# Attention scores of neighbouring blocks in two PSUM banks, the odd one with its heads' partition halves exchanged

## The chip, the cores and the metric

The kernel runs on one core of a Trainium2 chip. The metric is the time of one execution in microseconds of the device. Three runs of the kernel before took 499.46, 500.41 and 501.45 us; the median is 500.41 us.

## The reference

```python
# attention: 4 batches, 8 heads, 576 positions, 64 features a head
scores = scale * np.matmul(q, k.transpose(0, 1, 3, 2))
mask_plain = (rel >= 0) & (rel < 32)                          # heads 0 to 3
mask_dil = (rel >= 0) & (rel < 128) & (rel % 4 == 0)          # heads 4 to 7
scores = np.where(masks, scores, -1e9)
attn = softmax(scores); attn_out = attn @ v
# dense layer on the 2304 tokens of 512 features
h = x @ w_in; g = h - np.tanh(h); x = g @ w_out
# soft mixture of 8 experts with 4 slots each
logits = x @ phi
slot_input = softmax(logits, axis=0).T @ x
slot_out[e] = np.maximum(slot_input[e] @ w1[e], 0) @ w2[e]
out = softmax(logits, axis=1) @ slot_out
```

All data are float32. (`softmax` stands here for the subtraction of the maximum, exp, and the division by the sum plus 1e-9.)

## The kernel before

Everything runs in an order written out by hand: each engine executes its instructions in the order in which the program emits them. TensorE (PE) multiplies, ScalarE (ACT) and VectorE (DVE) read the results out of PSUM, GpSimd (POOL) works on SBUF alone, and all DMAs are issued from the SP queue.

**Attention.** The windows are narrow, so only blocks of the score matrix are computed. A step `i` handles a pair of heads (p) and a third (u) of their positions: 12 steps a batch, `PO = (2, 3, 0, 1)`, so the six dilated steps come first and the six plain ones after. A dilated step has 4 blocks of 48 queries by 80 keys, a plain step 3 blocks of 64 by 96 (`shape`, L279). One step passes through

- `emit_qk` (L247): transposes of q and k (L267) and their copies into `qk`, several of them for each pair of heads;
- `emit_scores` (L283): for each block c and each head x of the pair one matmul (L305). Head x has its 64 features in partitions 64x to 64x+63 and puts its scores into the same half of the partitions of one PSUM tile; the blocks lie side by side in the columns. For batches 0 and 1 (`by_pe`, `MASKPE = 2`) one bf16 matmul (L291) has put the mask there first and L305 adds to it, and the maximum (L314) and exp (L317, one ACT instruction a block, which also reads out the row sums) read PSUM. For batches 2 and 3 DVE adds the mask on the way to SBUF (L311), and the maximum and exp read SBUF;
- `emit_norm` (L323): reciprocals of the sums on DVE (L326, L328) and a multiplication on POOL (L329);
- `emit_trans` (L332): one transpose a block (L338) and a copy to SBUF by ACT (L97);
- `emit_pv` (L343): the product with v (L359, two column halves, one for each head), then ACT casts it to `xhi` (L97), DVE subtracts to get `xlo` (L391), and some tiles leave a remainder that is copied (L97).

**PSUM.** The pool `ps_m` has five banks under the tag `mm`; `mm(shape)` (L78) takes one of them. q/k transposes, scores, score transposes, products with v, transposes of g and several smaller things all go through these five. `ps_h` has two banks for h.

**Dense layer.** h of a chunk of 512 tokens (here: of a batch) is made of three products in fp32r for each quarter of the features (L503 to L505), then tanh on ACT (L509), a subtraction on DVE (L512), the logits (L518, four tiles of 32 output partitions) and a transpose of g (L537).

**Order.** Batches 0 and 1 of attention, the conversion of the weights (POOL L430, DVE L441 to L446, PE L468 to L492) and the first chunk of h are sorted by due times that stand at the top of the file; this fills the time to about 157 us. Extra matmuls (`warm`, L195) stand behind the first four scores. Then chunks 1 to 3 follow in a loop over eight pairs s of feature tiles. Attention of batch 2 is laid into chunk 1 and that of batch 3 into chunk 2 by the class `Attn`, pair by pair: `turn(s)` emits q/k transposes and the score transposes of the pair before, `score` the scores of steps 2s and 2s+1, `norms` their normalisation, and `values(s)` the products with v of the steps 2s-2 and 2s-1:

```python
                emit_tanh(pb, gs[b])
                if an:
                    an.score(2 * s)
                emit_sub(pb, gs[b])
                if an:
                    an.score(2 * s + 1)
                    an.norms(s)
                    an.values(s)
```

After that come the experts.

Of the kernel before, what the change touches and what calls it, by code (L numbers as in the profile page):

```python
# [13 lines left out]
ACTF = mybir.ActivationFunctionType  # L14
ALU = mybir.AluOpType
AX = mybir.AxisListType
# [43 lines left out]
def moe_kernel(ctx: ExitStack, tc: tile.TileContext, q, k, v, w_in, w_out, phi, w1, w2, out):  # L60
    nc = tc.nc
# [16 lines left out]
    def mm(shape):  # L78
        return ps_m.tile(shape, F32, tag="mm", name="mm")
# [46 lines left out]
    id2 = cpart(64).bitcast(BF16)[0:64].rearrange("p (a k) -> p a k", a=2)  # L126
# [156 lines left out]
    def emit_scores(b, i):  # L283
        p, u = PO[i // 3], i % 3
        nb, nq, nk = shape(i)
        ps = mm([128, nb, nk])
        mask = mask_d[:, (0, 4, 2)[u]:(4, 8, 6)[u]] if nb == 4 else mask_p[:, min(u, 1):min(u, 1) + 3]
        by_pe = b < MASKPE
        nr = nq if by_pe else 64
        if by_pe:  # L290
            nc.tensor.matmul(  # L291
                ps.rearrange("p c k -> p (c k)"), lhsT=id2.rearrange("p a k -> p (a k)"),
                rhs=mask[0:64].rearrange("p c k -> p (c k)"), start=True, stop=True,
            )
        for c in range(nb):
            for x in range(2):
                if nb == 4:

                    r2, qi = divmod(2 * u + c // 2, 3)
                    q0 = 288 * (c % 2) + 144 * r2  # L300
                    q0, k0 = q0 + nq * qi, q0 + max(0, nq * qi - 32)
                else:
                    q0, k0 = nq * (nb * u + c), max(0, nq * (nb * u + c) - 32)
                r = slice(64 * x, 64 * x + 64)
                nc.tensor.matmul(  # L305
                    ps[64 * x:64 * x + nr, c, :], lhsT=qT[b, p][r, q0:q0 + nr], rhs=kT[b, p][r, k0:k0 + nk],
                    start=not by_pe, stop=True, skip_group_check=True,
                )
        pr = prs.next()[:, 0:nb * nk].rearrange("p (c k) -> p c k", c=nb)
        if not by_pe:  # L310
            nc.vector.tensor_tensor(out=pr, in0=ps, in1=mask, op=ALU.add)  # L311
            ps = pr
        nm = tiny("nm", 4, 3)[:, 0:nb]
        nc.vector.tensor_reduce(out=nm, in_=ps, op=ALU.max, axis=AX.X, negate=True)  # L314
        sm = tiny("smm", 4, 3)[:, 0:nb]
        for c in range(nb):
            nc.scalar.activation(  # L317
                out=pr[:, c, :], in_=ps[:, c, :], func=ACTF.Exp, bias=nm[:, c:c + 1],
                accum_out=sm[:, c:c + 1],
            )  # L320
        sc_s[b, i] = (pr, sm)
# [21 lines left out]
    def emit_pv(b, i):  # L343
        p, u = PO[i // 3], i % 3
        nb, nq, nk = shape(i)
        if i == 0:
            xhi[b] = unit("xhi", [128, KT, 512], F32R)
            xlo[b] = unit("xlo", [128, KT, 512], F32R)
        pt = sc_pt.pop((b, i))
        o = mm([128, 192])  # L350
        for n0 in range(nb):
            for hh in range(2):
                if nb == 4:
                    m, x = divmod(n0, 2)
                    r2, qi = divmod(2 * u + m, 3)
                    n, c, col = 3 * (2 * r2 + x) + qi, 2 * m + hh, 96 * x + nq * m
                else:
                    n, c, x, col = nb * u + n0, n0, hh, nq * n0
                nc.tensor.matmul(  # L359
                    o[64 * hh:64 * hh + 64, col:col + nq], lhsT=vt[b, p](n, hh),  # L360
                    rhs=pt[:, c, 64 * x:64 * x + nq], start=True, stop=True,
                )
        hi, lo, rem = xhi[b][:, p, :], xlo[b][:, p, :], xrem[:, p, 64 * b:64 * b + 64]
        pieces, rems = [], []
        if p >= NP // 2:
            if u == 0:
                halves2 = lambda t: t.rearrange("p (l y) -> p l y", l=2)
                pieces.append((halves2(o), lambda t: halves2(t[:, 0:288])[:, :, 0:96]))
            elif u == 1:
                pieces.append((  # L370
                    o.rearrange("p (l m i) -> p m l i", l=2, m=2),
                    lambda t: t[:, 96:480].rearrange("p (m l i) -> p m l i", m=2, l=4)[:, :, ::3, :],
                ))
            else:
                pieces.append((o[:, 0:96], lambda t: t[:, 336:432]))
                pieces.append((o[:, 96:128], lambda t: t[:, 480:512]))
                rems.append((o[:, 128:192], rem))
        else:
            ov = o.rearrange("p (i r) -> p r i", r=4)
            pieces.append((ov[:, 0:3, :], lambda t: t[:, 0:432].rearrange("p (r i) -> p r i", r=3)[:, :, 48 * u:48 * u + 48]))  # L380
            if u == 0:
                pieces.append((ov[:, 3, :], lambda t: t[:, 432:480]))
            elif u == 1:
                pieces.append((ov[:, 3, 0:32], lambda t: t[:, 480:512]))
                rems.append((ov[:, 3, 32:48], rem[:, 0:16]))
            else:
                rems.append((ov[:, 3, :], rem[:, 16:64]))
        for src, f in pieces:
            copy(ENGS["hi"][min(b, 2)], f(hi), src)
        for src, f in pieces:  # L390
            nc.vector.tensor_tensor(out=f(lo), in0=src, in1=f(hi).bitcast(F32), op=ALU.subtract)  # L391
        for src, dst in rems:
            copy(ENGS["rem"][min(b, 2)], dst, src)
# [379 lines left out]
    with tc.manual_schedule():  # L773
# [71 lines left out]
        for ch in range(1, 4):  # L845
# [13 lines left out]
            for s in range(NFT // 2):  # L859
                a, b = 2 * s, 2 * s + 1  # L860
                pa, gs[a] = emit_h(xh, xl, a), gring.next()
                emit_tanh(pa, gs[a])
                emit_sub(pa, gs[a])

                if s:
                    emit_gT(ch, a - 2, gs[a - 2])
                    emit_gT(ch, a - 1, gs[a - 1])
                elif ch > 1:
                    last_posts()
                if s or ch == 1:  # L870
                    sm_one()
                if an:
                    an.turn(s)
                pb, gs[b] = emit_h(xh, xl, b), gring.next()
                emit_tanh(pb, gs[b])
                if an:
                    an.score(2 * s)
                emit_sub(pb, gs[b])
                if an:
                    an.score(2 * s + 1)  # L880
                    an.norms(s)
                    an.values(s)
                if s:
                    emit_logits(ch, a - 1, gs[a - 1])
                emit_logits(ch, a, gs[a])
                sm_one()
                room[0] += sum(ROOM.get((ch, f), 0) for f in (a, b))
                load_experts()
# [183 lines left out]
```

## Time and profile before

| what | value |
| --- | --- |
| median of three runs | 500.41 us (499.46 to 501.45) |
| the profiled execution | 501.07 us, span 499.3 us |
| TensorE busy | 470.8 us (94% of the span) |
| DVE, ACT, POOL busy | 222.9, 236.0, 83.6 us |
| L305, score matmuls | 672 instructions, mean 254 ns each, 36.0 us busy |
| mean granted TensorE clock | 0.96 |

The profile is of one execution. Times are in us from the start of the span; L305 is line 305 of the kernel. Matmuls overlap each other, so the time of one matmul is its latency; what a group costs is seen where the chain that ended last runs through it. PE is the matmul side of TensorE, PEld its weight loads. The granted clock is the share of the full TensorE clock.

### The profile page before, as it was taken

The numbers are of one execution on the slowest core, as the hardware profiler recorded it, in microseconds if no ns is written. First come the engines' busy times: TensorE is split into PE (matmuls) and PEld (weight loads), VectorE is DVE, ScalarE is ACT, GpSimd is POOL, SyncE is SP. The second block draws the span as 40 slices with busy tenths as digits, with TensorE's granted clock in tenths as the row PEclk, the third lists the DMA queues.
The fourth block names the chain that finished last, engine by engine and source line by source line (L and its number), as shares of the span: only waits on it lengthen the run. The fifth ranks groups of instructions, "written<-read, shape, count | busy, mean of one in ns | idle before, by whom it ended". The sixth has DMA issues, their size and how long they took to land.

```text
span 499.3 us, 11253 instructions
## 1 busy us (share of the span) xinstructions
PE 470.8 (94%) x4531; PEld 351.4 (70%) x4531; DVE 222.9 (45%) x558; ACT 236.0 (47%) x763; POOL 83.6 (17%) x99
## 2 busy tenths in 40 slices
PE   6989888999999999999999899999999999999981
PEld 4767676877777867888787678877678869845430
DVE  1787888954754445543252454332221223232132
ACT  3857536575655464665365356543132323313121
POOL 3463444432341010111011011100000000010000
PEclk9967768999999999999999999999999999999996
DMA  9997799444145401222320100209600259899938
GB/s 247 277 262 258 258 336 269 151 117 121 35 139 123 96 3 39 76 59 49 81 44 1 37 1 2 86 4 390 254 29 0 85 180 402 304 389 410 409 146 334
DMA packets 60740, 81.14 MB, mean 163 GB/s; under 512 B 35600, under 2 KB 39440, under 8 KB 60688
## 3 DMA queue, kind: packets, MB, share of 16 engines
q1 hardware_dynamic: 60688, 80.42, 49.7%
q8 instruction: 36, 0.59, 0.5%
q14 instruction: 16, 0.13, 0.1%
HBM read 71.50 MB, written 8.91 MB: 161 GB/s over the span
## 4 chain that ended last, share of the span: by engine, by line
PE 85%; DVE 6%; ACT 4%; issue 1%; DMA 1%; POOL 0%; POOLq 0%; ACTq 0%; DVEq 0%
PE h L503 14%; PE h L505 13%; PE h L504 13%; PE mm L305 6%; PE mm L537 5%; PE lg L518 4%; PE mm L359 4%; PE mm L338 4%; PE mm L635 3%; PE mm L267 3%; PE h L686 3%; PE y L711 3%; ACT mem L317 2%; PE warm L200 1%; PE mm L468 1%; PE mm L479 1%
## 5 line engine op out<-in xcount | busy, mean ns | idle before, releaser
L503 PE MATMUL h<-xhi,whi 128*128 128x512 f32 x256 | 107.1, 418 | 0.0
L505 PE MATMUL h<-xhi,wlo 128*128 128x512 f32 x256 | 101.0, 395 | 0.0
L504 PE MATMUL h<-xlo,whi 128*128 128x512 f32 x256 | 100.8, 394 | 0.0
L509 ACT ACTIVATE mem<-h 128x512 f32<-128x512 f32 x56 | 33.4, 596 | 83.7 <-PE h L505 83.7
L512 DVE TENSOR_TENSOR mem<-h,mem 128x512 f32<-128x512 f32 x56 | 38.6, 689 | 73.6 <-ACT mem L509 73.4
L329 POOL TENSOR_TENSOR mem<-mem 128x320 f32<-128x320 f32 (+1 forms) x48 | 34.5, 718 | 195.7 <-DVE mem L328 132.7
L503 PEld LDWEIGHTS h<-xhi,whi 128*128 128x128 f32 x256 | 48.8, 191 | 13.3 <-issue 5.0
L505 PEld LDWEIGHTS h<-xhi,wlo 128*128 128x128 f32 x256 | 48.5, 189 | 10.9
L504 PEld LDWEIGHTS h<-xlo,whi 128*128 128x128 f32 x256 | 48.9, 191 | 8.4
L97 ACT COPY g<-mm 128x512 f32<-128x512 f32 x72 | 40.2, 596 | 12.0 <-PE mm L550 4.8
L317 ACT ACTIVATE mem<-mm,mem 128x80 f32<-128x80 f32 (+1 forms) x84 | 26.8, 330 | 30.1 <-DVE mem L314 30.1
L305 PE MATMUL mm<-qk 64*64 64x96 f32 (+2 forms) x672 | 36.0, 254 | 2.1 <-DVE qk L97 2.0
L317 ACT ACTIVATE mem<-mem 128x80 f32<-128x80 f32 (+1 forms) x84 | 29.9, 357 | 16.5 <-DVE mem L314 14.5
L305 PEld LDWEIGHTS mm<-qk 64*64 64x64 f32 (+1 forms) x672 | 29.0, 139 | 10.6 <-issue 5.6
L97 ACT COPY mem<-mm 80x448 f32<-80x448 f32 (+4 forms) x64 | 26.7, 442 | 10.1 <-DVE xlo L391 6.5
L338 PE MATMUL mm<-mem 112*80 112x112 f32 (+1 forms) x168 | 25.4, 279 | 5.0 <-POOL mem L329 2.8
L311 DVE TENSOR_TENSOR mem<-mm,mem 128x320 f32<-128x320 f32 (+1 forms) x24 | 11.3, 470 | 41.8 <-PE mm L305 41.8
L512 DVE TENSOR_TENSOR gr<-h,gr 128x512 f32<-128x512 f32 x16 | 11.1, 691 | 42.2 <-ACT gr L509 42.2
L359 PEld LDWEIGHTS mm<-mem,v 80*64 80x64 f32 (+1 forms) x672 | 23.8, 144 | 7.8 <-issue 4.2
L359 PE MATMUL mm<-mem,v 80*64 80x48 f32 (+1 forms) x672 | 28.6, 234 | 0.0
L267 PE MATMUL mm<-mem,rqk 96*128 96x96 f32 x192 | 23.2, 262 | 5.1 <-DMA rqk<-in_k_dram 4.1
L460 POOL TENSOR_TENSOR wlo<-cvb,whi 128x512 fp32r<-128x512 f32 x16 | 21.5, 1343 | 38.0 <-DVE whi L97 14.4
(153 smaller groups left out, 749.3 us busy)
## 6 DMA issues: line engine op xcount, KB each, us to landing
ex<-in_moe_w_dram SPq DMA_DIRECT2D x30, 1024.0 KB, 10.6
raww<-in_moe_w_out_dram SPq DMA_DIRECT2D x8, 1024.0 KB, 8.7
raww<-in_moe_w_in_dram SPq DMA_DIRECT2D x8, 1024.0 KB, 5.9
wo_dram<-cva SPq DMA_DIRECT2D x16, 256.0 KB, 5.1
wo<-wo_dram SPq DMA_DIRECT2D x4, 1024.0 KB, 5.8
out_dram<-o SPq DMA_DIRECT2D x8, 512.0 KB, 4.8
v<-in_v_dram SPq DMA_DIRECT2D x24, 160.0 KB, 3.9
v<-in_v_dram SPq DMA_DIRECT2D x16, 192.0 KB, 3.4
```

Source lines behind the costliest of these rows:

```text
L97: (nc.scalar.copy if eng == "A" else nc.vector.tensor_copy)(out=out, in_=in_)
L267: nc.tensor.transpose(ps[:, r, :], raw[:, 3 * th + r if p < NP // 2 else 2 * r + th], ident[0:96, 0:96])
L305: nc.tensor.matmul(ps[64 * x:64 * x + nr, c, :], lhsT=qT[b, p][r, q0:q0 + nr], rhs=kT[b, p][r, k0:k0 + nk], start=not by_pe, stop=True, sk ...
L317: nc.scalar.activation(out=pr[:, c, :], in_=ps[:, c, :], func=ACTF.Exp, bias=nm[:, c:c + 1], accum_out=sm[:, c:c + 1],)
L329: nc.gpsimd.tensor_tensor(out=pr, in0=pr, in1=rc.unsqueeze(2).to_broadcast([128, nb, nk]), op=ALU.mult)
L338: nc.tensor.transpose(ps[:, c, :], pr[0:P, c, :], ident[0:P, 0:P])
L359: nc.tensor.matmul(o[64 * hh:64 * hh + 64, col:col + nq], lhsT=vt[b, p](n, hh), rhs=pt[:, c, 64 * x:64 * x + nq], start=True, stop=True,)
L503: nc.tensor.matmul(ps, lhsT=wh, rhs=xh[:, kt, :], start=(kt == 0), stop=False)
L504: nc.tensor.matmul(ps, lhsT=wh, rhs=xl[:, kt, :], start=False, stop=False)
L505: nc.tensor.matmul(ps, lhsT=wl, rhs=xh[:, kt, :], start=False, stop=(kt == KT - 1))
L509: nc.scalar.activation(out=g, in_=ps, func=ACTF.Tanh)
L512: nc.vector.tensor_tensor(out=g, in0=ps, in1=g, op=ALU.subtract)
```

## The change

A score now takes two PSUM tiles: even blocks go to the first, odd blocks to the second. In the second, head 0 writes the upper half of the partitions and head 1 the lower half (`o = 64 * (x ^ (c % 2))`). The product with v reads odd blocks accordingly. The mask matmul, the addition of the mask and, in batches 0 and 1, the maximum are each done once a tile; exp goes through the even blocks first. In chunks 1 and 2 the products with v are emitted ahead of the pair's scores, except at s = 1.

```diff
     def emit_scores(b, i):
         p, u = PO[i // 3], i % 3
         nb, nq, nk = shape(i)
-        ps = mm([128, nb, nk])
+        pss = [mm([128, (nb + 1 - y) // 2, nk]) for y in range(2)]
         mask = mask_d[:, (0, 4, 2)[u]:(4, 8, 6)[u]] if nb == 4 else mask_p[:, min(u, 1):min(u, 1) + 3]
         by_pe = b < MASKPE
         nr = nq if by_pe else 64
         if by_pe:
-            nc.tensor.matmul(
-                ps.rearrange("p c k -> p (c k)"), lhsT=id2.rearrange("p a k -> p (a k)"),
-                rhs=mask[0:64].rearrange("p c k -> p (c k)"), start=True, stop=True,
-            )
-        for c in range(nb):
-            for x in range(2):
...
+            for y, ps in enumerate(pss):
                 nc.tensor.matmul(
-                    ps[64 * x:64 * x + nr, c, :], lhsT=qT[b, p][r, q0:q0 + nr], rhs=kT[b, p][r, k0:k0 + nk],
-                    start=not by_pe, stop=True, skip_group_check=True,
+                    ps, lhsT=id2.rearrange("p a k -> p (a k)"), rhs=mask[0:64, y::2], start=True, stop=True,
                 )
+        for c0 in range(0, nb, 2):
+            for c in range(c0, min(c0 + 2, nb)):
+                for x in range(2):
...
+                    r = slice(64 * x, 64 * x + 64)
+                    o = 64 * (x ^ (c % 2))
+                    nc.tensor.matmul(
+                        pss[c % 2][o:o + nr, c // 2, :], lhsT=qT[b, p][r, q0:q0 + nr], rhs=kT[b, p][r, k0:k0 + nk],
+                        start=not by_pe, stop=True, skip_group_check=True,
+                    )
         pr = prs.next()[:, 0:nb * nk].rearrange("p (c k) -> p c k", c=nb)
         if not by_pe:
-            nc.vector.tensor_tensor(out=pr, in0=ps, in1=mask, op=ALU.add)
-            ps = pr
+            for y in range(2):
+                nc.vector.tensor_tensor(out=pr[:, y::2], in0=pss[y], in1=mask[:, y::2], op=ALU.add)
+            pss = [pr[:, y::2] for y in range(2)]
         nm = tiny("nm", 4, 3)[:, 0:nb]
-        nc.vector.tensor_reduce(out=nm, in_=ps, op=ALU.max, axis=AX.X, negate=True)
+        for src, dst in zip([pr], [nm]) if not by_pe else [(pss[y], nm[:, y::2]) for y in range(2)]:
+            nc.vector.tensor_reduce(out=dst, in_=src, op=ALU.max, axis=AX.X, negate=True)
         sm = tiny("smm", 4, 3)[:, 0:nb]
-        for c in range(nb):
+        for c in [*range(0, nb, 2), *range(1, nb, 2)]:
             nc.scalar.activation(
-                out=pr[:, c, :], in_=ps[:, c, :], func=ACTF.Exp, bias=nm[:, c:c + 1],
+                out=pr[:, c, :], in_=pss[c % 2][:, c // 2, :], func=ACTF.Exp, bias=nm[:, c:c + 1],
                 accum_out=sm[:, c:c + 1],
             )
...
                 nc.tensor.matmul(
                     o[64 * hh:64 * hh + 64, col:col + nq], lhsT=vt[b, p](n, hh),
-                    rhs=pt[:, c, 64 * x:64 * x + nq], start=True, stop=True,
+                    rhs=pt[:, c, 64 * (x ^ (c % 2)):64 * (x ^ (c % 2)) + nq], start=True, stop=True,
                 )
...
                 emit_tanh(pb, gs[b])
                 if an:
+                    if s > 1:
+                        an.values(s)
                     an.score(2 * s)
                 emit_sub(pb, gs[b])
                 if an:
                     an.score(2 * s + 1)
                     an.norms(s)
-                    an.values(s)
+                    if s == 1:
+                        an.values(s)
```

## Rows read from the trace of the kernel before

**Rows 1.** The page, part 4: shares of the chain that ended last.

```profile
PE 85%; DVE 6%; ACT 4%; issue 1%; DMA 1%; POOL 0%; POOLq 0%; ACTq 0%; DVEq 0%
```

**Rows 2.** Stretches: us; busy (count) of PE, PEld, DVE, ACT, POOL; clock; DMA; GB/s.

```profile
27.00:43.00 16.00, 14.62 (x136) 10.59 (x135) 11.53 (x27) 9.76 (x35) 8.40 (x10) 0.57 0.93 287
43.00:56.00 13.00, 11.91 (x177) 8.85 (x173) 11.48 (x33) 9.28 (x42) 4.18 (x5) 1.00 0.68 233
81.00:100.00 19.00, 19.00 (x190) 15.38 (x189) 18.20 (x29) 11.42 (x37) 10.01 (x9) 1.00 0.67 173
170.00:196.00 26.00, 25.19 (x263) 18.76 (x259) 12.58 (x35) 15.05 (x54) 2.89 (x4) 1.00 0.10 22
196.00:240.00 44.00, 44.00 (x494) 36.39 (x493) 19.50 (x59) 26.66 (x100) 5.45 (x8) 1.00 0.22 55
```

**Rows 3.** Chain that ended last, in time: start us, us, engine, tile, line, count.

```profile
35.34 1.15 PE mm L305 x12
...
46.11 0.64 PE mm L305 x12
...
51.52 0.64 PE mm L305 x12
...
90.96 0.69 PE mm L305 x16
...
160.41 0.36 PE lg L518 x8
...
183.56 0.57 PE lg L518 x16
...
196.77 1.25 PE mm L305 x32
198.02 1.07 PE mm L359 x32
...
207.53 1.14 PE mm L305 x24
...
219.20 0.85 PE mm L359 x24
```

**Rows 4.** Groups by line and shape: out<-in, count | busy us, mean ns | idle before.

```profile
L311 DVE TENSOR_TENSOR mem<-mm,mem 128x320 f32<-128x320 f32 x12 | 5.8, 486 | 20.7 <-PE mm L305 20.7
L311 DVE TENSOR_TENSOR mem<-mm,mem 128x288 f32<-128x288 f32 x12 | 5.4, 453 | 21.1 <-PE mm L305 21.1
...
L359 PEld LDWEIGHTS mm<-mem,v 80*64 80x64 f32 x384 | 13.4, 144 | 3.7 <-issue 1.9 <-DVE mem L326 0.4 <-ACT g L97 0.4
...
L291 PEld LDWEIGHTS <-mem 64*128 64x128 bf16 x24 | 2.3, 94 | 5.0 <-issue 4.8
```

**Rows 5.** Timeline of pairs 2, 3 and 5 of batch 2: start, us, instruction [idle before].

```profile
198.63 0.36 ACT L317 ACTIVATE mem<-mem 128x80 f32<-128x80 f32 x1 [1.23 <-DVE mem L314]
...
202.29 0.72 POOL L329 TENSOR_TENSOR mem<-mem 128x320 f32<-128x320 f32 x1 [0.86 <-DVE mem L328]
...
202.41 0.21 ACT L97 COPY mem<-mm 128x64 f32<-128x64 f32 x1 [0.51 <-DVE xlo L391]
...
203.74 0.78 PEld L338 LDWEIGHTS mm<-mem 112*80 112x80 f32 x8
...
212.55 0.67 POOL L329 TENSOR_TENSOR mem<-mem 128x288 f32<-128x288 f32 x1 [0.74 <-ACT xhi L97]
...
214.49 0.82 PE L338 MATMUL mm<-mem 128*96 128x128 f32 x6
...
232.84 0.67 POOL L329 TENSOR_TENSOR mem<-mem 128x288 f32<-128x288 f32 x1 [0.74 <-DVE mem L328]
...
234.09 0.82 PE L338 MATMUL mm<-mem 128*96 128x128 f32 x6
```

**Rows 6.** Timeline of POOL, 10 to 62 us: start, us, instruction [idle before].

```profile
22.08 1.05 POOL L430 TENSOR_TENSOR cva<-raww,mem 128x512 f32<-128x512 f32 x1 [3.03 <-DMA raww<-in_moe_w_out_dram]
...
28.34 0.72 POOL L329 TENSOR_TENSOR mem<-mem 128x320 f32<-128x320 f32 x1
```

More of the change, by code (lines that the diff above doesn't have):

```diff
@@ L290, in emit_scores @@
         if by_pe:
-            nc.tensor.matmul(
-                ps.rearrange("p c k -> p (c k)"), lhsT=id2.rearrange("p a k -> p (a k)"),
-                rhs=mask[0:64].rearrange("p c k -> p (c k)"), start=True, stop=True,
-            )
-        for c in range(nb):
-            for x in range(2):
[L297 to L304, printed above, removed]
+            for y, ps in enumerate(pss):
@@ L305, in emit_scores @@
                 nc.tensor.matmul(
-                    ps[64 * x:64 * x + nr, c, :], lhsT=qT[b, p][r, q0:q0 + nr], rhs=kT[b, p][r, k0:k0 + nk],
-                    start=not by_pe, stop=True, skip_group_check=True,
-                )
+                    ps, lhsT=id2.rearrange("p a k -> p (a k)"), rhs=mask[0:64, y::2], start=True, stop=True,
+                )
+        for c0 in range(0, nb, 2):
+            for c in range(c0, min(c0 + 2, nb)):
+                for x in range(2):
+                    if nb == 4:
+                        r2, qi = divmod(2 * u + c // 2, 3)
+                        q0 = 288 * (c % 2) + 144 * r2
+                        q0, k0 = q0 + nq * qi, q0 + max(0, nq * qi - 32)
+                    else:
+                        q0, k0 = nq * (nb * u + c), max(0, nq * (nb * u + c) - 32)
+                    r = slice(64 * x, 64 * x + 64)
[4 more added lines that the diff above has]
+                    )
```

## The prediction

> **What bounds the kernel now.** I read the chain of waits first: TensorE (PE) carries 85% of it, DVE 6%, ACT 4% [rows 1]. Then the table by stretch, to see where PE really is the limit [rows 2]: from 81 to 100 and from 196 to 240 us it is busy all the time at full clock (2.4 GHz); from 27 to 43 us it has gaps and the granted clock is 0.57, mostly its lower level (1.2 GHz); from 43 to 56 us DVE is nearly as busy as PE. So a shorter score stage is worth its full length only where nothing else waits beside PE.
>
> What one score costs is read from the chain's pieces [rows 3]. Each block and head leaves two matmul instructions, so a dilated score (four blocks) has 16 and a plain one (three) 12. From 16 to 32 instructions the time goes from 0.69 to 1.25 us: 35 ns each, 70 ns a pair for 80 columns. From 12 to 24 it goes from 0.64 to 1.14 us: 84 ns a pair for 96 columns. Both are 0.87 ns a column, so the two heads run side by side and the columns are the limit. At the lower clock a plain score takes 1.15 us, 0.51 more: its columns take twice as long. L518 has four tiles of 32 output partitions: 8 more instructions cost 0.21 us, 105 ns for four of 128 columns, 0.82 ns a column. So four tiles can run side by side too. L359 (48 columns, 64 weight columns) needs at most 67 ns a pair (1.07 us for 16), so pairs can follow closer than 70.
>
> **The change part by part.**
> *Four quarters.* An even and an odd block run together, so eight instructions take the time of four. Dilated: half of 0.56, so 0.28 us saved (0.55 at the lower clock). Plain: the third block stays alone, a third of 0.50, so 0.165 us (0.33). Gross: batch 0 has two dilated scores at the lower clock, four at the upper, three plain at each: 1.1 + 1.1 + 1.0 + 0.5 = 3.7 us. Batch 1 has one dilated at the lower clock, five at the upper, six plain: 0.55 + 1.4 + 1.0 = 2.95. Batches 2 and 3: 2.7 each. Together 12.0 us. That the four quarters overlap is not shown before; the bounds are 0 and 12.0. I take 12.0, because L359 (two tiles with the same input rows) and L305 (different rows) each show one half of it, and L518 four at once [rows 3].
>
> *Mask.* Two matmuls over half the columns replace one, 24 times. The columns are the same. Lower bound 0 (the second weight load hides behind the first matmul), upper bound the whole 94 ns weight load of L291 [rows 4]; I take a third, 30 ns, since other weight loads mostly hide: 0.35 us for each of batches 0 and 1.
>
> *Split DVE work.* From 288 to 320 elements L311 goes from 453 to 486 ns [rows 4]: 1.03 ns an element plus 157. Two halves of 160 take 644 ns, 0.16 more. In batches 2 and 3 that is the add, in 0 and 1 the reduction, where the next instruction overlaps some of it; I take 0.1 us there.
>
> *Values ahead of scores.* This touches pairs 2 to 5 of batches 2 and 3. Before, with L305 from 196.77, exp starts at 198.63, and POOL ends the second normalisation at 203.01; the second score's transposes need it at about 204.1 (half of 0.78 after 203.74): 1.1 us to spare [rows 5]. Behind the waiting transposes stands all of PE's queue, the next h first. Now PE runs L359 first (1.07 us). ACT puts the xhi casts in its wait before exp, and DVE the xlo subtractions. The first add then comes 1.07 - 0.28 later from PE, about 0.45 more because DVE, in order, has to do both tiles' xlo first, and these pass to and fro between ACT and DVE (one such handover now makes ACT wait 0.51), and 0.2 for the split: 1.45 us. Transposes are wanted 0.55 earlier. Stall: 1.45 + 0.55 - 1.1 = 0.9 us. The three later pairs, by the same working: 1.07 - 0.165, then 0.85 - 0.165 twice (L359 of plain heads, 0.85 [rows 3]), plus 0.05, 0.1 and 0.35 for the handovers (fewer where a tile leaves no remainder), plus 0.15: late by 1.1, 0.95 and 1.2. To spare the third pair has 214.49 + 0.41 - 213.22 = 1.65, the fifth 234.09 + 0.41 - 233.51 = 1.0, the fourth as much as the fifth [rows 5]. With 0.33 gained each, the stalls are 0, 0.3 and 0.55. Stalls 1.75 against gains 0.55 + 3 x 0.33 = 1.54: +0.2 a batch. The first pair gains nothing, since PE already waits there for ACT (25.19 of 26.00 us busy in 170 to 196 us). Of the second pair's 0.55 I book half. Batches 2 and 3 come to about 0.
>
> *Batch 0.* What is gained before 29 us meets POOL, which waits for a weight DMA until 22.08, then goes from one thing to the next to the normalisation at 28.34 to 29.06, for which PE's transposes wait [rows 6]. Only the six plain scores after it count: 3 x 0.33 + 3 x 0.165 = 1.5, less 0.2 mask and 0.5 for DVE, which is the fuller one from 43 us on: 0.8.
> *Batch 1.* 2.95 less 0.35 mask, less 0.3 where DVE is at 18.20 of 19.00 us: 2.3.
> *Banks.* A score takes two of the five mm banks. From 46.11 to 51.52 us three plain scores come 2.7 us apart [rows 3]; one holds its bank for 0.64, a DVE pass of 0.45 and three exps of 0.36, 2.2 us or more, while four other tiles come by. DVE covers a PE wait there; uncovered it costs up to 0.5 us a score, 3 us over six.
>
> Sum: -0.8 - 2.3 + 0 = -3.1. The profiled execution took 501.07 us (span 499.3, 1.8 around it), so 498.0; it stood 0.66 above the median of 500.41, which gives **497.3 us**. A measurement of this kernel tells 0.5%, 2.5 us, from no change.
>
> **The rivals.**
> *A, the sum*, 497.3, own range 495.5 to 499.5. Chance 0.45, of which 0.33 is below 497.9.
> *B, the normalisation comes too late* (slower). Place: L338 waiting for L329 in pairs 2 to 5 of batches 2 and 3. It breaks even when POOL is about 1.15 us later than now; each further us is paid in full, eight times. If the xhi, remainder and xlo handovers between ACT and DVE take 1 us more than I booked, the stalls are 1.9, 0.8, 1.3 and 1.55, 5.5 a batch, less 1.54: +8 in all, with -3.1 from batches 0 and 1: 505. For it: ACT waits 0.51 us for DVE within one L359 tile [rows 5]. Against: ACT has 1.23 us free before exp. Chance 0.14.
> *C, the quarters don't overlap.* Then the change doesn't do what it says: mask 0.7, banks 0.5, and stalls of 0.6, 0, 0.2 and 0.4 without gains, 2.4 for two batches: 504. Against: L359 does a pair in 67 ns or less while one weight load lasts 144 ns [rows 3, 4], and both of its tiles take all rows, so weights load while a matmul on the same rows runs. The Trainium skill (TensorE: Matmul & The Clock Gate, Part 3, The mechanism) says that a weight load overlaps matmuls in flight only where the row group differs; odd blocks share the row group of even ones, so by that rule this rival would be the likely one. The trace disagrees with it at L359. Chance 0.08.
> *D, all passes.* The chains of batches 2 and 3 have more to spare than I read, and batch 0 keeps 2 us: 3.1 + 1.2 + 4 = 8 saved, 492. Chance 0.13.
> *E, the banks.* PE waits for a bank wherever scores come close and gives back batches 0 and 1; or PE, done sooner, has longer gaps and falls to half clock once more (0.64 against 1.15 us for a plain score). 500.4. Chance 0.20, all within 0.5%.
>
> **How the numbers follow.** Faster: 0.33 of A and D, 0.46. Within: 0.12 of A and E, 0.32. Slower: B and C, 0.22. The range takes in A and E, half of D and the lower part of B and C: 492.5 to 503.5.
>
> **What would show it.** L305's 32 instructions in about 0.7 us, 24 in about 0.8; if they stay at 1.25 and 1.14, C. L338 waiting for L329 for some tenths of a us in pairs 2, 4 and 5: A; one us or more in each: B; none: D. PE's idle before L291 and L305, with exp or a copy as its releaser: E. Batch 1 (77 to 157 us) should shrink by some 2 us, batch 0's end hardly move. The forecast is wrong if the stretch from 157 to 335 us changes by more than 2 us either way.

## The result, and the profile after

The changed kernel took 504.68 us (median of 4 runs, 504.20 to 505.00) beside 500.35 us for the kernel before in the same series (4 runs, 499.46 to 501.45): ratio 1.0094 [1.0074, 1.0115]. It was forecast at 497.3 us, so the sign was wrong. The profiled execution took 504.35 us, its span 502.2 us at a mean granted clock of 0.951 (before: 501.07, 499.3 and 0.96).

The page of the changed kernel, part 4, shares of the chain that ended last:

```profile
PE 67%; DVE 11%; DMA 8%; ACT 7%; issue 3%; POOL 2%; POOLq 0%; ACTq 0%
```

TensorE carried 85% of the chain before [rows 1] and now carries 67%; the rest went to DVE, ACT, POOL and DMA. The share alone does not tell the time: e1 and e7 below are equally fast (496.34 and 496.45 us) at 79% and 71%. The next question is whether the scores became shorter at all. The chain of the changed kernel, its pieces at the score line L309 (L305 before), in the columns of [rows 3]:

```profile
26.12 0.71 PE mm L309 x16
31.55 0.83 PE mm L309 x12
...
228.68 1.04 PE mm L309 x24
...
265.66 0.71 PE mm L309 x32
```

They did. 32 instructions take 0.71 us where they took 1.25, and 12 at the lower clock 0.83 where they took 1.15 [rows 3]. The four quarters of the array run side by side, as booked (0.54 us saved for two dilated scores, 0.56 forecast). The 24 instructions at 228.68 stand at 1.04 against 1.14; that group holds a wait, to which the experiments come back (0.81 in e9 below, where it holds none).

The stretches of the changed kernel, columns as in [rows 2], and after them two stretches of the kernel before that [rows 2] do not have:

```profile
12.00:27.00 15.00, 12.00 (x171) 8.60 (x169) 11.10 (x26) 10.02 (x40) 7.49 (x10) 0.88 1.19 266
27.00:43.00 16.00, 16.00 (x159) 11.83 (x153) 12.73 (x34) 10.01 (x35) 9.46 (x12) 0.50 0.96 284
43.00:56.00 13.00, 13.00 (x129) 10.34 (x131) 7.92 (x25) 8.08 (x33) 3.33 (x4) 0.58 0.67 232
81.00:100.00 19.00, 17.69 (x187) 13.96 (x186) 17.36 (x32) 11.54 (x37) 9.49 (x8) 0.99 0.83 230
196.00:240.00 44.00, 43.00 (x491) 34.35 (x490) 19.27 (x65) 27.08 (x100) 5.45 (x8) 1.00 0.20 53
275.00:285.00 10.00, 8.27 (x60) 5.93 (x54) 3.07 (x7) 2.79 (x5) 0.00 (x0) 0.83 0.20 44
```

```profile
12.00:27.00 15.00, 14.32 (x201) 11.44 (x200) 11.68 (x27) 11.19 (x47) 8.14 (x12) 1.00 1.20 271
275.00:285.00 10.00, 8.25 (x102) 6.01 (x94) 4.17 (x10) 2.99 (x6) 0.00 (x0) 1.00 0.21 45
```

From 12 to 27 us TensorE is busy for 12.00 us instead of 14.32. Then it runs at the half clock through 27 to 43 us (0.50, before 0.57), and for most of 43 to 56 us, where the kernel before had the full clock [rows 2]. PE busy for all of 16.00 us there is no sign of good use: at 1.2 GHz a plain score took 1.15 us before, at 2.4 GHz 0.64 [rows 3]. A second, short fall of the clock stands at 275 to 285 us. The timeline of the changed kernel shows where batch 0 waits, first a row of POOL, then one of PE, and last the same transposes in the kernel before:

```profile
23.00 1.04 POOL L436 TENSOR_TENSOR cva<-raww,mem 128x512 f32<-128x512 f32 x1 [4.65 <-DMA raww<-in_moe_w_out_dram]
```

```profile
24.77 0.97 PE L344 MATMUL mm<-mem 112*80 112x112 f32 x4 [2.40 <-POOL mem L335]
```

```profile
23.94 0.55 PE L338 MATMUL mm<-mem 112*80 112x112 f32 x4 [0.39 <-POOL mem L329]
```

POOL waits for the weights 4.65 us instead of 3.03 [rows 6], its normalisation comes behind that conversion, and PE's transposes wait 2.40 us for it instead of 0.39. That one profile does not make the longer wait the change's doing. In e1 it is 2.88 us, and e1 ends batch 0 earlier than the kernel before; in the eight profiles without quarters there (before, e2, e3, e8, e9, e11, e12, e13) it is 0.39 to 2.71 us. In all fifteen profiles these transposes start between 23.2 and 25.2 us.

To place the loss I follow the 72 tanh instructions (L509 before, L515 after, on ACT) in the timelines: one ends each block of h, so the start of the n-th, less its start before, is the lead (minus) or lag at that point, in us. Batch 2 lies between tanh 16 and 31, batch 3 between 32 and 46. The columns e1 to e9 are experiments told below.

| tanh (start before) | changed | e5 | e1 | e2 | e3 | e4 | e6 | e9 |
|---|---|---|---|---|---|---|---|---|
| 0 (70.70) | +1.26 | +0.36 | -1.92 | +0.77 | -1.41 | -0.84 | -2.37 | -2.39 |
| 3 (89.11) | +0.78 | -0.79 | -2.30 | +0.81 | -1.33 | -2.00 | -2.37 | -3.82 |
| 4 (96.23) | +1.82 | +0.29 | -1.22 | +0.82 | -1.33 | -0.92 | -1.45 | -3.82 |
| 16 (165.92) | +0.15 | -1.34 | -2.84 | +0.78 | -1.37 | -2.55 | -1.45 | -3.82 |
| 31 (245.68) | +0.64 | -0.87 | -4.59 | +1.53 | -0.86 | -2.55 | -1.44 | -5.60 |
| 36 (271.25) | -0.05 | -1.56 | -5.28 | +1.53 | -1.55 | -2.55 | -1.45 | -6.28 |
| 37 (283.11) | +1.52 | +0.03 | -5.30 | +1.53 | -1.56 | -0.95 | -1.48 | -6.31 |
| 46 (329.35) | +2.28 | +0.82 | -6.52 | +2.27 | -0.76 | -0.93 | -1.48 | -7.51 |

Read the first column downwards. 1.26 us are lost by the end of batch 0, another 1.04 in one step between tanh 3 and 4, 1.67 regained in the rest of batch 1 (tanh 4 to 16), 0.49 lost in batch 2 and 1.64 in batch 3, of which 1.57 in one step between tanh 36 and 37 (the short fall of the clock). Behind the last row the span loses another 0.7 (2.9 in all), which e5's does not. The first row is not settled by one profile: e2 and e3 run the same instructions as the kernel before up to 165 us, and their tanh 0 stand at +0.77 and -1.41. Differences down a column are much firmer than the first entry.

The scatter at the top goes with the clock. Five profiles run the same instructions up to 165 us: the kernel before, e2, e3, e9 and e12. Up to tanh 3 they spend 30.7, 34.1, 27.3, 10.2 and 23.9 us at the half clock (added up from the granted clock of each trace), and their tanh 3 stand at 0, +0.81, -1.33, -3.82 and -1.04: about 0.19 us for each us at the half clock. The changed kernel has 37.5 us there, e5 30.7 and e1 27.3. Which of the two makes the other, these profiles don't show.

### The profile page after: what moved, and what is told of

It reads as the page before. It is cut to its first block, busy times and chain, and to the rows that moved or that the text cites. A ratio compares the mean times of both kernels' runs of the same rounds, so it can differ in the third digit from the quotient of the medians.

```text
span 502.2 us, 11371 instructions
## 1 busy us (share of the span) xinstructions
PE 467.1 (93%) x4555; PEld 344.6 (69%) x4555; DVE 226.1 (45%) x606; ACT 238.3 (47%) x763; POOL 83.6 (17%) x99
## 4 chain that ended last, share of the span: by engine, by line
PE 67%; DVE 11%; DMA 8%; ACT 7%; issue 3%; POOL 2%; POOLq 0%; ACTq 0%
PE h L509 12%; PE h L511 11%; PE h L510 11%; PE mm L543 4%; DMA ex<-in_moe_w_dram 4%; PE lg L524 4%; PE mm L365 4%; PE mm L344 3%; PE mm L641 3%; PE mm L309 3%; ACT mem L323 3%; PE mm L267 3%; PE h L692 2%; DMA raww<-in_moe_w_out_dram 2%; DMA rqk<-in_k_dram 2%
## 5 line engine op out<-in xcount | busy, mean ns | idle before, releaser
L509 PE MATMUL h<-xhi,whi 128*128 128x512 f32 x256 | 107.2, 419 | 0.0
L515 ACT ACTIVATE mem<-h 128x512 f32<-128x512 f32 x56 | 33.3, 595 | 86.2 <-PE h L511 86.1
L335 POOL TENSOR_TENSOR mem<-mem 128x320 f32<-128x320 f32 (+1 forms) x48 | 34.5, 720 | 197.6 <-DVE mem L334 130.7
L509 PEld LDWEIGHTS h<-xhi,whi 128*128 128x128 f32 x256 | 49.0, 191 | 13.4 <-issue 5.0
L397 DVE TENSOR_TENSOR xlo<-mm,xhi 128x144 fp32r<-128x144 f32 (+4 forms) x72 | 17.0, 269 | 51.3 <-ACT xhi L97 44.9
L344 PE MATMUL mm<-mem 112*80 112x112 f32 (+1 forms) x168 | 27.9, 292 | 7.0 <-POOL mem L335 4.7
L543 PE MATMUL mm<-mem 128*128 128x128 f32 x192 | 27.6, 281 | 1.4 <-ACT mem L323 1.2
L515 ACT ACTIVATE gr<-h 128x512 f32<-128x512 f32 x16 | 9.6, 600 | 38.3 <-PE h L511 38.3
L309 PE MATMUL mm<-qk 64*64 64x96 f32 (+2 forms) x672 | 26.9, 265 | 0.8 <-DVE qk L97 0.3
```

Source lines behind the costliest of these rows:

```text
L309: nc.tensor.matmul(pss[c % 2][o:o + nr, c // 2, :], lhsT=qT[b, p][r, q0:q0 + nr], rhs=kT[b, p][r, k0:k0 + nk], start=not by_pe, stop=True, ...
L344: nc.tensor.transpose(ps[:, c, :], pr[0:P, c, :], ident[0:P, 0:P])
L509: nc.tensor.matmul(ps, lhsT=wh, rhs=xh[:, kt, :], start=(kt == 0), stop=False)
L515: nc.scalar.activation(out=g, in_=ps, func=ACTF.Tanh)
L543: nc.tensor.transpose(ps[:, j, :], g[:, 128 * j:128 * j + 128], ident)
```

## The experiments

All runs, with the median of the runs of the kernel before that shared their chip. The ratios, with their 95% intervals, are not the quotients of the medians. Clock is the median over the runs of the mean granted clock.

| | kernel | median us (range, runs) | clock | before | ratio |
|---|---|---|---|---|---|
| e1 | values late | 496.34 (494.46 to 499.72, 8) | 0.959 | 500.31 | 0.9938 [0.9904, 0.9972] |
| e2 | values first, no quarters | 502.71 (500.37 to 503.27, 7) | 0.962 | 500.31 | 1.0048 [1.0024, 1.0072] |
| e3 | quarters in batches 2, 3 | 499.66 (496.21 to 503.63, 12) | 0.975 | 500.31 | 0.9987 [0.9960, 1.0014] |
| e4 | quarters in batches 0, 1 | 500.84 (499.28 to 503.36, 12) | 0.956 | 500.31 | 1.0011 [0.9988, 1.0034] |
| e5 | the changed kernel again | 500.95 (500.21 to 504.24, 8) | 0.959 | 499.77 | 1.0045 [1.0026, 1.0064] |
| e6 | two banks, no exchange, late | 502.39 (497.42 to 506.90, 12) | 0.967 | 499.77 | 1.0026 [0.9998, 1.0054] |
| e7 | e1 with the wait filled | 496.45 (494.79 to 497.56, 6) | 0.963 | 499.77 | 0.9948 [0.9933, 0.9963] |
| e8 | late, quarters in 1, 2, 3 | 495.35 (493.85 to 498.63, 6) | 0.968 | 499.77 | 0.9925 [0.9899, 0.9950] |
| e9 | late, quarters in 2, 3 | 495.81 (493.38 to 500.46, 7) | 0.967 | 500.03 | 0.9926 [0.9886, 0.9966] |
| e10 | before, fewer dummies | 500.32 (498.33 to 503.10, 12) | 0.959 | 500.03 | 1.0010 [0.9984, 1.0036] |
| e11 | e8, wrong conversion moved | 495.76 (494.80 to 498.26, 6) | 0.968 | 500.84 | 0.9902 [0.9870, 0.9934] |
| e12 | e9, values first in pair 3 | 497.13 (495.29 to 501.69, 12) | 0.968 | 500.84 | 0.9934 [0.9906, 0.9962] |
| e13 | e8, right conversion moved | 495.51 (494.37 to 497.51, 10) | 0.964 | 499.51 | 0.9914 [0.9884, 0.9945] |

The 94 runs of the kernel before beside these are a measurement of their own. Their mean clock lies between 0.953 and 0.981 and their time follows it (correlation -0.89): 498.7 us in the median of the 34 runs at 0.970 or more, 501.3 of the 30 runs from 0.957 to 0.964, 503.7 of the 6 runs below 0.955. A straight line through them falls by 2.2 us for each 0.01.

**e5: is the number itself repeatable?**

> The changed kernel itself once more, beside the kernel before on this chip. Up to 165 us its instructions are those of the run with the values late (e1), whose profile was 2.84 us ahead of before there, while the first profile of the changed kernel was 0.15 us behind, with 38 us instead of 27 us at the half clock up to 81 us. Theory P (the place of the half-clock stretches differs from run to run by luck): the clock scatters as in e1 (0.951 to 0.968), the median is e1's plus the 4.3 us that the values cost in batches 2 and 3: about 500.5 us, no different from before, and the 504.7 us of the first four runs had unlucky clocks. Theory S (the clock of this program is lower by nature): 504 to 505 us again at a clock of 0.95.

The median was 500.95 us, ratio 1.0045: theory P held, though the kernel is still slightly slower than before. Seven of the eight runs had a clock of 0.959 to 0.966 and took 500.21 to 502.5 us; the eighth had 0.949 and took 504.24. All four runs of the first series had 0.949 to 0.951. So 504.7 us is this kernel at a low clock, and about 501 us is what it took in the second series. Why four runs in a row had the low clock stays open.

**e1: the values behind the scores again.**

```diff
-                    if s > 1:
-                        an.values(s)
                     an.score(2 * s)
...
-                    if s == 1:
-                        an.values(s)
+                    an.values(s)
```

> The changed kernel with the values behind the scores in every pair, as before; the quarters and the second bank stay in all four batches. Theory V (the move of the values costs what the quarters save in batches 2 and 3): without it each pair keeps its 0.55 or 0.33 us, 2.6 us a batch, where the changed kernel lost 0.5 and 1.6 us: 504.7 - 2.1 - 5.2 = about 497.5 us, and the transposes (L344) of the pairs wait for nothing. Theory W (the waits and the clock: TensorE, done sooner, waits longer for POOL at 22 to 25 us and for the pairs, and runs at the half clock for longer): the move has little part in it, the time stays at 503 to 505 us, with stretches at 1.2 GHz as long as in the changed kernel (about 38 us up to 81 us). Theory D (the split VectorE and mask instructions of the second bank): also 503 to 505 us, with exps (L323) late behind VectorE in every pair.

It took 496.34 us: theory V. From tanh 16 to 46 it gains 3.68 us, where the changed kernel lost 2.13 and e5 2.16, of which 1.57 and 1.59 are the clock's step at tanh 37. So the move costs about 4.2 us: 3.68 + 0.56. What of the page shows it is pair 4 of batch 2. Timeline of PE, the changed kernel and then e1 (the line numbers of e1 are 2 higher):

```profile
218.61 1.15 PE L309 MATMUL mm<-qk 64*64 64x96 f32 x24
...
223.99 1.09 PE L344 MATMUL mm<-mem 128*96 128x128 f32 x6
```

```profile
214.10 0.88 PE L311 MATMUL mm<-qk 64*64 64x96 f32 x24
...
220.06 0.82 PE L346 MATMUL mm<-mem 128*96 128x128 f32 x6
```

Neither row of the changed kernel has a bracket with a wait, yet each group is 0.27 us longer: the wait sits inside the group. In pair 2 of batch 3 a score's group is cut by it, so that it has a bracket:

```profile
286.87 0.49 PE L309 MATMUL mm<-qk 64*64 64x80 f32 x12 [0.26 <-DVE xlo L397]
```

The score waits until DVE has emptied a bank of the values. For the transposes, the chain of pair 4 names the work:

```profile
218.47 0.30 ACT xhi L97 x2
...
219.02 0.21 DVE xlo L397 x2
...
219.53 0.44 DVE mem L316 x2
...
222.06 1.20 ACT mem L323 x6
...
223.82 0.68 POOL mem L335
...
224.55 0.53 PE mm L344 x3
```

With the values first, their eviction (xhi on ACT, xlo on DVE) goes ahead of the score's add on DVE. Add, exps and normalisation come later, and the second half of the transposes (x3) waits for POOL. In e1 the chain from 196 to 206 us, around pair 2, is PE alone.

**e2: the move alone, in the kernel before.**

```diff
                 if an:
+                    if s > 1:
+                        an.values(s)
                     an.score(2 * s)
...
-                    an.values(s)
+                    if s == 1:
+                        an.values(s)
```

> The kernel before with the values ahead of the scores in pairs 2 to 5 of batches 2 and 3, and nothing else: one bank, halves not exchanged. Theory V: the scores come later by the values' 0.85 to 1.07 us and the exps, the normalisation and the transposes with them, with no shorter scores to make up for it: L338 waits for POOL L329 by over 1 us in pairs 2, 4 and 5 and the time is 504 to 507 us. Theories W and D: the move is all but free, 500 to 501.5 us.

502.71 us, ratio 1.0048, between the two. Theory V is right in kind and too large: without any quarters the move costs 0.75 us in batch 2 (tanh 16 to 31) and 0.74 in batch 3, and PE's only bracket with the normalisation in batch 2 stands in pair 5 (0.26 us). In pair 2 the eight transposes take 1.14 us instead of 0.93: a wait inside the group.

**e3 and e9: quarters in batches 2 and 3 alone, values first and values late.** Both have one bank and no exchange in batches 0 and 1:

```diff
+BANKS = (1, 1, 2, 2)
...
-        pss = [mm([128, (nb + 1 - y) // 2, nk]) for y in range(2)]
+        ny = BANKS[b]
+        pss = [mm([128, (nb + ny - 1 - y) // ny, nk]) for y in range(ny)]
...
-                    o = 64 * (x ^ (c % 2))
+                    o = 64 * (x ^ (c % BANKS[b]))
```

> Second bank and exchanged halves in batches 2 and 3 alone, with the values first there; batches 0 and 1 as before. The granted clock of batches 0 and 1 should be that of the kernel before (30.7 us at the lower level up to 81 us). Theory V: batches 0 and 1 were neutral in the changed kernel (1.5 us lost by 100 us, 1.35 us regained by 161 us), so the time stays at 504 to 505 us. Theory W: a good part of the loss starts in batch 0, so it falls to 501.5 to 503 us.

> Second bank and exchanged halves in batches 2 and 3 alone, values late: batches 0 and 1 are those of the kernel before. If the parts add up (3.7 us from batches 2 and 3, read off e1's tanh times between 166 and 329 us, with nothing from the rest): 496 to 497 us, and against e3 (the same with the values first) the move alone is worth 3 to 4 us. If the gain of e1 in batches 2 and 3 depended on what batches 0 and 1 did: 499 us or more.

e3 took 499.66 us, ratio 0.9987, so neither theory's number; but its clock was 0.975. From tanh 16 to 46 it loses 0.61 us, as the changed kernel does without the clock's step (0.56). e9 took 495.81, ratio 0.9926, and gains 3.69 us over the same stretch: with the values late, batches 2 and 3 alone bring all that e1 brings. Between the two the move is worth 3.85 us by the medians and 4.3 by the tanh starts.

**e12: the move in pair 3 alone.**

```diff
-                    if s > 1:
+                    if s == 3:
                         an.values(s)
...
-                    if s == 1:
+                    if s != 3:
                         an.values(s)
```

> Second bank and exchanged halves in batches 2 and 3, values ahead of the scores in pair 3 of each alone. By the working of the prediction pair 3 loses nothing by the move (its exps are late by 1.1 us and have 1.65 us to spare): 495 to 496.5 us, as e9, and the two pairs 3 take the same time as in e9. Rival (the move costs about the same in every pair, 3.85 us over eight pairs): 0.5 us a pair, 496.5 to 497.5 us.

The median was 497.13 us at a ratio of 0.9934, e9's being 0.9926: the median lies in the rival's range, but by the ratios no difference can be told. The tanh starts tell it: pair 3 of batch 2 (tanh 23 to 25) gains 0.35 us in e12 and 0.35 in e9, and 46 stands 3.64 against 3.69 us ahead of 16. The move is free where the exps have 1.65 us to spare. The cost lies in the pairs that have less.

**e4, e8, e7 and e10: batches 0 and 1.** e4 has `BANKS = (2, 2, 1, 1)` and e8 `BANKS = (1, 2, 2, 2)`, both with the values late. e7 is e1 with two more steps in the plan of batch 0, and e10 the kernel before with fewer dummies:

```diff
+                if b == 0 and i == NWARM:
+                    at(t + WAT * dt, warm, 5)
+                    at(t + 0.66 * dt, warm, 4)
```

```diff
-NWARM = 4
+NWARM = 1
```

> Second bank and exchanged halves in batches 0 and 1 alone; batches 2 and 3 as before, values behind the scores. Theory V: 500 to 501 us, since batches 0 and 1 came out at +0.15 us by 161 us. Theory W: 501.5 to 503 us, the longer time at the half clock (23 to 54 us) not made good.

> Values late, second bank and exchanged halves in batches 1, 2 and 3 alone. By the profiles so far batch 1 regains 1.65 us from 96 us on and batches 2 and 3 3.7 us: 495 us if batch 0 itself brings nothing (its waits eat the gain), 496.5 to 498 us if batch 0's quarters bring the 1.4 us by which the first tanh of e1 stands ahead of the run without them there.

> e1 (quarters everywhere, values late) with 18 more dummy matmuls (warm) in batch 0: ten behind the scores of unit 4, eight ahead of the transposes of unit 3, where TensorE otherwise waits 0.57 and 2.40 us. Theory W (that wait is what lets the clock fall at 23 us): the clock stays whole beyond 27 us, batch 0 ends earlier, 493.5 to 495.5 us at a clock of 0.965 or more. Rival (the weights' transfer sets the pace of batch 0 whatever the clock): no change, 496 to 497 us.

> The kernel before with the dummy matmuls (warm) behind the scores of units 1 to 3 of batch 0 left out (NWARM 1 instead of 4): only TensorE's filling between 12 and 20 us is less. Theory W (emptier stretches of TensorE in batch 0 lower the clock, and a lower clock costs what it costs between runs of one kernel, some 2.1 us for 0.01 of the mean): the mean clock falls from 0.967 to 0.955 or less and the time rises to 502 us or more. Rival (the transfers set the pace of batch 0 whatever the clock): the clock falls and the time stays at 499.5 to 501 us.

e4 took 500.84 us, ratio 1.0011: quarters in batches 0 and 1 bring nothing that can be measured. e8, e9 and e1 say the same from the other side (0.9925, 0.9926, 0.9938): batches 2 and 3 make the gain, and adding batch 1 and then batch 0 adds nothing that shows in the times. But the clock moved: the four kernels with quarters in batch 0 (e1, e4, e5, e7) have medians of 0.956 to 0.963, the rest but e10 0.962 to 0.975. The middle of the first is 0.959, of the others 0.967; by the line above, 0.008 less would be about 1.8 us, an estimate.

e7 filled the wait. Its stretches, to be held against the first two of the changed kernel:

```profile
12.00:27.00 15.00, 13.57 (x206) 10.48 (x205) 10.99 (x28) 10.01 (x40) 7.78 (x11) 1.00 1.19 264
27.00:43.00 16.00, 14.90 (x163) 10.48 (x162) 14.25 (x35) 11.28 (x44) 9.51 (x11) 0.68 0.94 271
```

The clock now holds up to 27 us and falls behind it, and 496.45 us is e1's time, the rival's number. But the half clock was moved more than removed (23.9 us up to tanh 3, in e1 27.3), so the run does not tell what a whole clock would be worth there. e10 took 30 dummy matmuls out of batch 0, some 3.8 us of PE (1.27 us for ten at full clock), and its clock fell by 0.008, but the time stayed at 500.32: the rival's number again, though it does not separate the two, since less work and a lower clock may have cancelled. Its profile points that way: with 34.1 us at the half clock its tanh 3 stands at -0.55, where 0.19 us for each us would put it at about +0.6. So that the transfers alone set the pace of batch 0 is not shown. They do set the transposes at 23.2 to 25.2 us, and DMA moves 260 to 292 GB/s from 12 to 43 us in every profile. But by tanh 3 the five profiles of the same instructions are 4.6 us apart, in step with the half clock.

**e6: the second bank without the exchange of halves**, values late:

```diff
-                    o = 64 * (x ^ (c % 2))
+                    o = 64 * x
...
-                    rhs=pt[:, c, 64 * (x ^ (c % 2)):64 * (x ^ (c % 2)) + nq], start=True, stop=True,
+                    rhs=pt[:, c, 64 * x:64 * x + nq], start=True, stop=True,
```

> The second bank with its split mask, add, max and exp order in all batches, but odd blocks keep the halves of even ones; values late. If the exchange is what lets blocks run side by side, the x32 group of scores takes 1.25 us as before, and the time against before is the bare price of the second bank: by the terms of the prediction (0.30 to 0.35 us a unit of batches 0 and 1 where nothing hides it, 0 in batches 2 and 3) 500 to 504 us. If two banks alone do it, the group takes 0.7 us and the time is e1's, 496 us.

The chain of e6 in batch 2 (L312 are its scores):

```profile
195.32 1.25 PE mm L312 x32
206.09 1.14 PE mm L312 x24
```

These are the times of the kernel before to the digit [rows 3]: the second bank alone does not make the overlap, the exchange on top of it does. The bare price of the bank reads off the tanh starts: 0.92 us in the step from tanh 3 to 4, and nothing over all of batches 2 and 3 (-1.45 to -1.48). By the times it is 1.0026 [0.9998, 1.0054]. The halves exchanged in a single bank were not tried, so whether the overlap needs the second bank stays open.

**e11 and e13: the step between tanh 3 and 4.** It is there in every kernel with a second bank in batch 1 (0.92 to 1.08 us) but e13, and in none without. PE's timeline in e8:

```profile
92.54 0.66 PE L545 MATMUL mm<-mem 128*128 128x128 f32 x4 [1.23 <-ACT mem L325]
```

The transposes of g wait for exps of a score: those exps free the bank that the transposes take. The chain of e8 shows what the exps wait for:

```profile
85.81 1.45 DVE cva L449
...
87.28 1.11 DVE cva L451
...
88.41 1.42 DVE cva L454
89.83 0.60 DVE mem L520
90.43 0.34 DVE cvb L449
...
90.80 0.69 DVE cvb L454
91.49 0.24 DVE mem L322
...
91.76 0.74 ACT mem L325 x4
...
92.54 0.66 PE mm L545 x4
```

DVE converts weights for 5 us before it gets to the max (L322). Both runs delay the last conversion (cvb, L449 and L454) of one column block past a max, e11 of block 6, e13 of block 5 (the edit of e13):

```diff
-            at(t + CB, conv_b, "in", e)
-            at(t + IC * dt, conv_in_c, e)
+            late_in = 0.8 if e == 5 else 0
+            at(t + CB + late_in, conv_b, "in", e)
+            at(t + IC * dt + 0.5 * late_in, conv_in_c, e)
```

> e8 (values late, quarters in batches 1, 2 and 3) with VectorE's conversion of one weight column block (1.03 us) moved from ahead of the max of one unit's scores, at 90.4 us, to behind it. Theory B (in that unit the second bank makes the transposes of g wait: their bank is the one that the unit's exps free, 1.23 us on TensorE at 92.5 us, and the exps wait for the max behind that conversion): the wait shrinks by about 1 us and tanh 5 stands about 1 us earlier against before than in e8, the time falls by as much, 494 to 495 us. Rival (the wait has another cause, or the later conversion makes a wait of its own): the step of about 1 us between tanh 3 and tanh 4 stays, 495 to 496 us.

> e8 with VectorE's conversion of the weight block that stands in the chain (cvb, 0.34 and 0.69 us at 90.4 us of e8, directly ahead of the max) moved behind that max. Theory B (the second bank makes the transposes of g wait for the exps of the same unit, and these wait for the max behind the conversion): the wait of 1.23 us at 92.5 us shrinks to 0.1 to 0.3 us, and the step of 1.04 us between tanh 3 and tanh 4 against before becomes 0 to 0.2 us; time 494 to 495.3 us. Rival (the bank is held by something else): the wait and the step stay, 495 to 496 us.

e11 was a miss of mine: block 6 belongs to the next unit, so the chain at 92 us was untouched, and its wait stayed at 1.23 us and its step at 1.06. e13 moved the right one. Chain and timeline of e13:

```profile
91.29 0.60 DVE mem L520
91.89 0.24 DVE mem L322
...
92.15 0.73 ACT mem L325 x4
...
92.93 0.66 PE mm L545 x4
```

```profile
92.93 0.66 PE L545 MATMUL mm<-mem 128*128 128x128 f32 x4 [0.17 <-ACT mem L325]
```

The wait is 0.17 us and the step -0.02: theory B is shown. The median, 495.51 us at 0.964, does not show it, because the clock scatters by more than 1 us' worth between the runs, and e13's profile had the short fall at tanh 37 (a step of 1.57 us) as well.

**The best version.** e8, e9, e11 and e13 lie between 495.35 and 495.81 us, within each other's intervals, 0.7 to 1.0% faster than the kernel before. e9 is the simplest of them: quarters in batches 2 and 3, values where they were.

## Why the prediction was wrong, by its own steps

Three steps of the sum failed. *Banks* was entered at 0 and cost 1.04 us in batch 1, the greater part of the 1.7 us by which batch 1 fell short. Batches 2 and 3 were entered at 0 and lost 0.56 us. And the clock was taken as that of the kernel before: it was 0.959 in e5 and 0.949 in the first series, by the line above some 1.8 and 4 us (estimates). With these, -3.1 + 1.7 + 0.6 + 1.8 gives +1.0 us, where e5 stands 1.2 above the kernel before; with 4 us for the clock it gives +3.2, where the first series stands 4.3 above, so about 1 us of that series stays open.

*Four quarters: right.* 0.71 and 0.83 us, as above. Rival C falls. e1 and e6 send the same sequence of input rows through the array and differ in the output partitions of the odd blocks alone, yet 32 instructions take 0.71 us in one and 1.25 in the other. The Trainium skill (TensorE: Matmul & The Clock Gate, Part 3, The mechanism) lets a weight load overlap matmuls in flight only where the row group differs; the trace disagrees with that here too, since the output halves alone make 0.71 out of 1.25 us.

*Mask: 0 instead of 0.35 us a batch.* At 96.76 us of e8 the two mask matmuls take 0.24 us in the chain, and the one before took 0.24 at 90.72 us. The second weight load is hidden whole there; the lower bound was the true one.

*Split DVE work: right in size* (two adds of 128x160 at 316 ns are 0.15 us more than one at 486 [rows 4]; 0.16 forecast).

*Batch 1: -2.3 forecast.* From tanh 4 on it gains 1.67 us in the changed kernel, but the step of 1.04 ahead of that is the term *Banks*, which was written down with its bounds of 0 and 3 us and entered in the sum at 0. Net -0.6. The place was foreseen only in kind: not a score that waits for a bank but the transposes of g, whose bank the exps of a score now hold.

*Batch 0: -0.8 forecast.* That the gains ahead of 29 us are absorbed is right: the transposes that wait for POOL start at 23.95 to 24.77 us in the five profiles with quarters in batch 0, and at 23.2 to 25.2 in the ten others. The six scores behind it were booked as gained, at the clock of before, and the times show nothing of that: batches 0 and 1 came out at 1.0011 [0.9988, 1.0034] (e4) where 3.1 us less, a ratio of 0.994, were forecast. The work may well be saved: set against 0.19 us for each us at the half clock, the tanh 3 of the five (changed, e1, e4, e5, e7) stand 0.5 to 1.6 us ahead, an estimate, while the profiles without quarters from which that slope comes lie within 0.7 us of it. The medians of the clock are lower with quarters in batch 0 (0.956 to 0.963), which would take it back; why they are lower stays open.

*Batches 2 and 3: about 0 forecast.* By tanh starts the changed kernel loses 0.49 us in batch 2 and 0.07 in batch 3 beside the clock's step (2.13 us with it, just over the 2 us that the prediction had named as its sign of being wrong). The working by pairs was nearly right (pair 3 has 1.68 us to spare by the rows shown, not 1.65): pairs 2 to 5 of batch 2 measured +0.30, -0.36, +0.21 and +0.66 us, against +0.35, -0.33, -0.03 and +0.22. The fourth and fifth were undersized by 0.2 and 0.4: the second score waits inside its group for the values' tiles to be evicted (1.15 us instead of 0.88), a wait that needs two banks for each score and the values ahead of them, and the prediction had the two in separate paragraphs. Rival B was right in its place, at a small part of its price (POOL L335 makes PE wait 0.30 and 0.56 us in pairs 2 and 5 of batch 2, and 0.58 us in pair 5 of batch 3).

*The clock: no term at all.* The sum was made at the clock of the profile of before, 0.96. Rival E named a mechanism (longer gaps, one more fall to the half clock) and 500.4 us. That e5 came so close, at 500.95 us, may be luck, since it is not shown that the gaps lower the clock. What no rival had was a run of runs at 0.949. Brought to the clock of before (0.967, with 2.2 us for 0.01, an estimate) and held against the runs of before beside it, e4 stands at -1.9 us, e3 at +1.0, e9 at -4.2, e1 at -5.8 and e5 at -0.6. The parts add up to within 0.3 us: e4 and e9 to e1, e4 and e3 to e5. (With means in place of medians the single numbers move by up to 0.8 us.) So the change as made is worth at most some 0.6 us at equal clock instead of 3.1, and loses 1.8 us (e5) to 4 us (first series, 0.949) to the clock. That line comes from runs of one kernel that differ in their clock; that the clock alone makes the whole difference is not shown (neither e7 nor e10 separates it).

## What to carry to other kernels

Before a faster instruction is booked as gained, look in the same stretch for what ends its engine's next wait: work taken from an engine that then waits for a transfer is worth nothing up to that wait, and here it went with a lower clock behind it. A reorder that comes with a speedup is an edit of its own, to be timed without it: here it cost some 4 us and hid a gain of 0.7%. Read the mean granted clock beside every time: two series of the changed kernel differed by 0.7%, at 0.949 and 0.959.

## What the hardware showed that I had not expected

Time and mean granted clock of one and the same program go together over 94 runs, 496.9 us at 0.981 and 506.18 at 0.954, without any difference in its instructions. With tiles of 64 input rows and 64 output partitions it matters that all four quarters differ: 32 instructions into two banks take 1.25 us with two quarters in turn and 0.71 with four. And between tanh 36 and 37, where PE waits twice for ACT (0.85 us ahead of L344 in the changed kernel, 0.87 ahead of L338 before), the clock fell for a moment in four of the profiles (changed, e4, e5, e13; 1.57 to 1.60 us each) and not in the others, with the same waits.
